# Routing of the last two batches in one pass: joint running maximum, one rescaling, one accumulated product

## The chip, the cores and the metric

The kernel runs on one core of a Trainium2 chip. The metric is the device time of one execution in microseconds. The kernel before takes 646.65 us, the median of three runs (645.55, 646.65, 647.51).

## The reference

Three layers in a row, all in float32. First a packed attention over 8 batches, 8 heads, 576 rows and head size 64: 32 packed queries attend to all rows, and then all rows attend to the 32 results. Then a soft mixture of 8 experts with 32 slots (4 per expert), and last a two-layer network with the activation h * tanh(softplus(h)). The change lies in the second layer, where the softmax of the logits runs over all 4608 rows, for each slot:

```
logits = x @ phi
d = logits - logits.max(0, keepdims=True)
d = np.exp(d)
d /= d.sum(0, keepdims=True) + 1e-09
slot_input = d.T @ x
```

After that each expert computes `relu(slot_input[e] @ w1[e]) @ w2[e]`, and the rows mix the slots by a softmax of the same logits over the 32 slots.

## The kernel before, in words

**Stages.** The kernel first does the attention batch by batch. The rows' logits of a batch (tile LT) come out of the attention weights A and a small product G of the packed values and phi, so the layer's input x is never formed. After the last batch the experts run one after the other (ex_h, ex_x, ex_o), with TensorE products of the slots against w1 and w2, then the last network over row blocks, which is the longest stage.

**Routing of a batch.** The sum over all rows is kept as a running one. For batch b the steps are: r_mx (maximum mc of LT per partition), r_mr (TensorE turns it into a row, mr), r_row (row maximum; nrep is the running negative maximum), r_d (TensorE copies it to the partitions, mp; ACT writes column b of nM), r_de (exponential dT and its sum sb), r_da (al, the factor by which older sums are rescaled), r_dt and r_dt_c (transposed dp, copied to Dt), r_u and r_u_c (product us with A, copied to up), r_sel and r_sel_c (uq, copied to U), r_si (product si with the packed values pp) and r_si_c (si_acc = al * si_acc + si). For the last batch r_last also forms the sum ss over partitions and its reciprocal rs, by which si_acc is scaled. si_acc is turned by TensorE (sit_ps) and copied to SIT, which the first expert product hp (line 986) reads.

**Order around the change.** All engines work in the order in which the kernel's code issues them (a manual schedule). The last two batches, x = 6 and y = 7, are written out as a list of calls. In it stand two kinds of filler. warm1(n) issues n products of the identity with itself, with no reader. bg(n) issues the next n steps of a fixed list: the conversion of eight w_in tiles, numbered 0 to 7, each of three steps (cv_z on ACT, line 280; cv_u on DVE, line 286; cv_m on DVE, line 289), whose results are kept in win.

**Transfers.** SP issues all weight loads in one fixed order into buffers that are used again; `done` after the last reader of a buffer lets the next load into it be written. A load waits on SP for the readers of its buffer, and the loads behind it wait with it. The buffers of w_in tiles 1 to 7 are taken, in this order, by two tiles of w1 of expert 3, four more w_in tiles and the first tile of w2 of expert 3. Behind these stand loads into the buffers of w1 of experts 0 and 1, and so on through the experts to the 16 tiles of w_out.

Of the kernel before, what the change touches and what calls it, by code (L numbers as in the profile page):

```python
# [9 lines left out]
F32 = mybir.dt.float32  # L10
F32R = mybir.dt.float32r
I32 = mybir.dt.int32
AF = mybir.ActivationFunctionType
ALU = mybir.AluOpType
# [5 lines left out]
def kernel(  # L20
# [13 lines left out]
    nc = tc.nc  # L34
    B, H, S, D = q.shape
# [269 lines left out]
    def bg(n):  # L305

        for _ in range(n):
            if bgq:
                bgq.pop(0)()
# [217 lines left out]
    def s2_mul(b, z):  # L527
        lo, hi = parts(b, z)
        A = v4(st[b]["A"][:, lo:hi])
        n = (hi - lo) * 4  # L530
        m = st[b].pop(("rs", z))
        nc.gpsimd.tensor_tensor(out=A, in0=A, in1=m[:, :, None].to_broadcast([128, n, J]), op=ALU.mult)

    def at(b, n):
        d = st[b]
        A = d["A"]
        if n == 0:
            AT = t1.tile([128, HQ, NB, 128], F32, name="AT", tag="eT", bufs=1)
            d["AT"] = AT.rearrange("p q i c -> p q (i c)")
        AT = d["AT"]  # L540
        if n < HQ:
            tp = ps_t.tile([128, 4, 128], F32, name="at", tag="t")
            for i in range(4):
                nc.tensor.transpose(tp[:, i], A[:, HQ * i + n], ident)
            nc.scalar.copy(out=AT[:, n, 0:512], in_=tp.rearrange("p i c -> p (i c)"))  # L545
            return
        rem = ps_t.tile([128, HQ, 64], F32, name="atr", tag="t")
        nc.tensor.transpose(rem.rearrange("p q c -> p (q c)"), A[:, 8], ident)
        nc.scalar.copy(out=AT[:, :, 512:576], in_=rem)
# [39 lines left out]
    def r_d(b):  # L589
        d = st[b]  # L590
        mp = ps_t.tile([128, 1], F32, name="mp", tag="t")
        nc.tensor.matmul(mp, lhsT=nrep.rearrange("p g m -> p (g m)"), rhs=ident[0:1, 0:1], start=True, stop=True)
        nc.scalar.copy(out=nM[:, b:b + 1], in_=mp)

    def r_de(b):
        d = st[b]
        dT = t1.tile([128, 192], F32, name="dT", tag="dT", bufs=1)
        sb = s_acc if b == 0 else t1.tile([128, 1], F32, name="sb", tag="sb")
        nc.scalar.activation(out=dT, in_=LT[:, b], func=AF.Exp, bias=nM[:, b:b + 1], scale=1.0, accum_out=sb)
        d["dT"] = dT  # L600
        d["sb"] = sb

    def r_da(b):
        d = st[b]
        if b:
            al = t1.tile([128, 1], F32, name="al", tag="al")
            nc.scalar.activation(out=al, in_=nM[:, b - 1:b], func=AF.Exp, bias=nM[:, b:b + 1], scale=-1.0)
            d["al"] = al

    def r_dt(b):  # L610
        d = st[b]
        dT = d.pop("dT")
        dp = ps_t.tile([128, NB, M], F32, name="dp", tag="t")
        nc.tensor.transpose(dp[:, 0:4].rearrange("p i m -> p (i m)"), dT[:, 0:128], ident)
        for hq in range(HQ):
            nc.tensor.matmul(dp[64 * hq:64 * hq + 64, 4], lhsT=dT[0:32, 128:192], rhs=ident[0:32, 0:32], start=True, stop=True)
        d["dp"] = dp

    def r_dt_c(b):
        d = st[b]  # L620
        dp = d.pop("dp")
        Dt = t1.tile([128, NB, M], F32, name="Dt", tag="Dt")
        nc.scalar.copy(out=Dt, in_=dp)
        d["Dt"] = Dt

    def r_u(b):
        d = st[b]
        A, Dt = d.pop("A"), d.pop("Dt")
        us = ps_t.tile([128, HQ * 128], F32, name="us", tag="t")
        for i in range(4):  # L630
            nc.tensor.matmul(
                us[32 * i:32 * i + 32], lhsT=Dt[:, i], rhs=A[:, HQ * i:HQ * i + HQ].rearrange("p q c -> p (q c)"),
                start=True, stop=False,
            )
        for i in range(4):
            r = slice(64 * (i // 2), 64 * (i // 2) + 64)
            nc.tensor.matmul(
                us[32 * i:32 * i + 32, 64 * i:64 * i + 64], lhsT=Dt[r, 4], rhs=A[r, 8, 64 * (i % 2):64 * (i % 2) + 64],
                start=False, stop=True,
            )  # L640
        d["us"] = us

    def r_u_c(b):
        d = st[b]
        us = d.pop("us")
        up = t1.tile([128, HQ * 128], F32, name="up", tag="up", bufs=1)
        nc.scalar.copy(out=up, in_=us)
        d["up"] = up

    def r_sel(b):  # L650
# [7 lines left out]
    def r_sel_c(b):  # L658
        d = st[b]
        uq = d.pop("uq")  # L660
        U = t1.tile([128, HQ * M], F32, name="U", tag="U")
        nc.scalar.copy(out=U, in_=uq)
        d["U"] = U

    def r_si(b):
        d = st[b]
        U, pp = d.pop("U"), d.pop("pp")
        si = ps_t.tile([128, HQ, D], F32, name="si", tag="t")
        for hq in range(HQ):
            for h4 in range(4):  # L670
                r = slice(32 * h4, 32 * h4 + 32)
                nc.tensor.matmul(si[r, hq], lhsT=U[r, hq * M:hq * M + M], rhs=pp[r, hq], start=True, stop=True)
        d["si"] = si

    def r_si_c(b):
        d = st[b]
# [11 lines left out]
    def r_last(b):  # L688

        d = st[b]  # L690
        al, sb = d.pop("al"), d.pop("sb")
        nc.vector.scalar_tensor_tensor(out=s_acc, in0=s_acc, scalar=al, in1=sb, op0=ALU.mult, op1=ALU.add)
        ss_ps = ps_t.tile([128, 1], F32, name="ss_ps", tag="t")
        nc.tensor.matmul(ss_ps, lhsT=idrep, rhs=s_acc, start=True, stop=True)
        rs = t1.tile([128, 1], F32, name="rs", tag="rs")
        nc.vector.tensor_scalar_add(out=rs, in0=ss_ps, scalar1=1e-9)
        nc.vector.reciprocal(out=rs, in_=rs)
        nc.vector.tensor_scalar(out=si_acc, in0=si_acc, scalar1=al, scalar2=rs, op0=ALU.mult, op1=ALU.mult)
        d["rs"] = rs
# [116 lines left out]
    def warm1(n):  # L816

        ps = ps_s1.tile([128, 2, 512], F32, name="s1", tag="s1")
        for _ in range(n):
            nc.tensor.matmul(ps[:, 0, 0:128], lhsT=ident, rhs=ident, start=True, stop=True)  # L820
# [67 lines left out]
    warm1(2)  # L888
    r_row(x)
    at(y, 1)  # L890
    s2_mul(y, 2)
    at(y, 2)
    r_d(x)
    bg(3)
    r_de(x)
    lt(y)
    lt_c(y)
    r_dt(x)
    warm1(4)
    r_dt_c(x)  # L900
    bg(1)
    bg(3)
    r_u(x)
    r_mx(y)
    r_mr(y)
    bg(1)
    bg(1)
    bg(1)
    warm1(4)
    warm1(1)  # L910
    r_u_c(x)
    bg(1)
    r_sel(x)
    warm1(2)
    r_sel_c(x)
    r_row(y)
    bg(1)
    bg(1)
    bg(1)
    r_d(y)  # L920
    r_da(x)
    r_si(x)
    r_de(y)
    bg(1)
    r_da(y)
    r_dt(y)
    r_dt_c(y)
    warm1(1)
    r_si_c(x)
    bg(2)  # L930
    bg(1)
    r_u(y)
    bg(1)
    r_u_c(y)
    warm1(2)
    r_last(y)
    r_sel(y)
    warm1(2)
    bg(1)
    r_sel_c(y)  # L940
    r_si(y)
    r_si_c(y)
    bg(1)


    sit_ps = ps_t.tile([128, 128], F32, name="sit_ps", tag="t")
# [592 lines left out]
```

## Time and profile before

| | before |
|---|---|
| median of three runs | 646.65 us |
| the profiled execution | 644.71 us, its span 642.9 us |
| mean granted TensorE clock in it | 0.989 of full |
| busy share of the span: PE, DVE, ACT, POOL | 95%, 78%, 53%, 9% |
| HBM read, written | 79.23 MB, 9.44 MB |

The span is cut by the profile into stages only through time: the join of the last two batches lies from about 145 to 163 us, the experts from there to about 222 us, the last network behind them. Busy shares are averages over these stages, so what an instruction costs is read in its own stretch: a timeline gives start and length of each instruction and, in brackets, how long its engine waited before it and for whom.

### The profile page before, as it was taken

Reading aid. Unit: us, or ns where it says so; the run is one execution under the profiler, and the core shown is the slowest. Engines: PE = TensorE matmul, PEld = TensorE weight load, DVE = VectorE, ACT = ScalarE, POOL = GpSimd, SP = SyncE. Lnnn points to the kernel's source line nnn. Section 1 sums busy time; section 2 is a strip of 40 time slices with the busy share of each in tenths; the row PEclk is TensorE's granted clock in tenths of the full one; section 3 lists DMA queues with packets and bytes.
Section 4 is the critical chain, followed back from the end, with each engine's and each line's share of the span. In section 5 each row is a group of like instructions: output and inputs, shape, how many; then the busy total and the mean of one; then the engine's idle time right before and its main releaser. Section 6 shows DMA issues by size and latency. Waiting matters only on the chain.

```text
span 642.9 us, 14422 instructions
## 1 busy us (share of the span) xinstructions
PE 611.3 (95%) x5874; PEld 528.6 (82%) x5874; DVE 501.1 (78%) x997; ACT 337.8 (53%) x681; POOL 55.2 (9%) x78
## 2 busy tenths in 40 slices
PE   7899999998998969999999999999999999999996
PEld 5777777776344548888899999999999999999996
DVE  5998888887564398988779987788778877887883
ACT  3345555646334367655456555555555555555551
POOL 5122222121020030010000000000000000000000
PEclk9899999998999979999999999999999999999999
DMA  8988955999999960020110110111011101110111
GB/s 283 344 292 292 343 174 199 405 413 396 360 410 412 412 223 1 1 53 14 33 34 2 34 34 2 35 34 34 2 34 34 34 2 34 34 34 2 34 34 34
DMA packets 42354, 89.61 MB, mean 139 GB/s; under 512 B 10928, under 2 KB 19248, under 8 KB 42288
## 3 DMA queue, kind: packets, MB, share of 16 engines
q1 hardware_dynamic: 41840, 88.36, 38.8%
q8 instruction: 46, 0.75, 0.5%
q10 hardware_dynamic: 192, 0.26, 0.2%
q14 instruction: 20, 0.16, 0.1%
q0 software_dynamic: 256, 0.07, 0.0%
HBM read 79.23 MB, written 9.44 MB: 138 GB/s over the span
## 4 chain that ended last, share of the span: by engine, by line
PE 65%; DVE 18%; DMA 8%; ACT 5%; issue 1%; SPq 1%; DVEq 0%; POOL 0%; ACTq 0%; POOLq 0%
PE o L1317 39%; PE so L1317 14%; DMA AW<-in_moe_w_dram 6%; PE h L1199 5%; DVE kT L335 4%; DVE A L507 1%; DMA r_wo<-in_moe_w_out_dram 1%; DVE mx L506 1%; PE s L487 1%; DVE AY L1358 1%; DVE S L1215 1%; DVE sm L522 1%; DVE nmx L383 1%; PE s L820 1%; ACT AT L545 1%
## 5 line engine op out<-in xcount | busy, mean ns | idle before, releaser
L1317 PE MATMUL o<-W,gh 128*128 128x256 f32 (+1 forms) x888 | 159.4, 306 | 0.5 <-DVE AY L1358 0.5
L1317 PEld LDWEIGHTS o<-W,gh 128*128 128x128 f32 x888 | 129.7, 190 | 10.0 <-issue 1.9
L1230 ACT CAST gh<-AY 128x512 fp32r<-128x512 f32 x116 | 53.8, 511 | 109.1 <-PE o L1317 109.1
L1204 ACT ACTIVATE AY<-h 128x512 f32<-128x512 f32 x132 | 77.1, 594 | 37.4 <-PE h L1199 36.0
L1317 PE MATMUL o<-W,gl 128*128 128x256 f32 (+1 forms) x444 | 94.3, 302 | 0.0
L1233 DVE TENSOR_TENSOR gl<-AY,gh 128x512 fp32r<-128x512 f32 x116 | 59.4, 553 | 33.0 <-ACT gh L1230 33.0
L1234 DVE TENSOR_TENSOR Sl<-S,Sh 128x1024 fp32r<-128x1024 f32 x58 | 70.9, 1223 | 10.4 <-ACT Sh L1231 9.0
L1317 PEld LDWEIGHTS o<-W,gl 128*128 128x128 f32 x444 | 70.7, 188 | 4.5
L1317 PE MATMUL o<-T,Sh 128*128 128x256 f32 x464 | 73.9, 281 | 0.4 <-DVE AY L1358 0.4
L1231 ACT CAST Sh<-S 128x1024 fp32r<-128x1024 f32 x58 | 60.8, 1049 | 5.6 <-DVE S L1215 4.3
L1317 PEld LDWEIGHTS o<-T,Sh 128*128 128x128 f32 x464 | 62.8, 189 | 0.6 <-DVE AY L1358 0.6
L1215 DVE TENSOR_TENSOR S<-AY 128x256 f32<-128x256 f32 x116 | 48.7, 420 | 9.9 <-ACT AY L1204 9.9
L1199 PE MATMUL h<-CS,W 128*128 128x256 f32 x288 | 55.7, 284 | 0.0
L1317 PE MATMUL o<-T,Sl 128*128 128x256 f32 x232 | 46.6, 282 | 0.0
L1199 PEld LDWEIGHTS h<-CS,W 128*128 128x128 f32 x288 | 43.9, 188 | 2.2 <-issue 0.7
L1358 DVE TENSOR_TENSOR AY<-AY,o 128x256 f32<-128x256 f32 x86 | 33.0, 417 | 9.4 <-PE o L1317 6.4
L1317 PE MATMUL so<-T,Sh 128*128 128x256 f32 (+1 forms) x232 | 38.7, 289 | 0.4 <-DVE AY L1358 0.4
L373 PE MATMUL s<-kT,win 128*128 128x288 f32 x128 | 34.7, 416 | 2.4 <-ACT win L385 2.3
L1317 PEld LDWEIGHTS o<-T,Sl 128*128 128x128 f32 x232 | 35.8, 190 | 0.0
L487 PE MATMUL s<-win,qT 128*128 128x128 f32 x256 | 33.7, 287 | 1.9 <-ACT win L353 1.9
L487 PEld LDWEIGHTS s<-win,qT 128*128 128x128 f32 x256 | 31.4, 200 | 2.8 <-issue 2.0
L1317 PEld LDWEIGHTS so<-T,Sh 128*128 128x128 f32 x232 | 32.5, 190 | 1.2 <-issue 0.6
(282 smaller groups left out, 1039.5 us busy)
## 6 DMA issues: line engine op xcount, KB each, us to landing
AW<-in_moe_w_dram SPq DMA_DIRECT2D x45, 512.0 KB, 10.2
r_wo<-in_moe_w_out_dram SPq DMA_DIRECT2D x16, 512.0 KB, 9.0
out_dram<-AY SPq DMA_DIRECT2D x64, 128.0 KB, 2.1
r_wi<-in_moe_w_in_dram SPq DMA_DIRECT2D x13, 512.0 KB, 8.8
AW<-in_q_dram SPq DMA_DIRECT2D x11, 576.0 KB, 5.2
AW<-in_k_dram SPq DMA_DIRECT2D x9, 576.0 KB, 7.3
AW<-in_v_dram SPq DMA_DIRECT2D x40, 128.0 KB, 5.6
AC<-in_moe_w_dram SPq DMA_DIRECT2D x10, 512.0 KB, 9.1
```

The costliest lines, as they stand in the source:

```text
L335: nc.vector.transpose(out=T[:, dh, main].rearrange("p (i r a) -> p a i r" if nm == "k" else "p (i a r) -> p a i r", i=4, a=4,), in_=x[:, 0 ...
L373: nc.tensor.matmul(ps[:, n, 0:288], lhsT=pBD[b % 2][:, hq, dh], rhs=kT[:, dh, 288 * n:288 * n + 288], start=(dh == 0), stop=(dh == 1),)
L487: nc.tensor.matmul(ps[:, k - lo], lhsT=d["qT", hq][:, dh, 64 + 128 * i:192 + 128 * i], rhs=ppBD[b % 2][:, hq, dh], start=(dh == 0), stop=( ...
L1199: nc.tensor.matmul(hp[:, 256 * f:256 * f + 256], lhsT=MS[:, 128 * ft:128 * ft + 128], rhs=CS[:, 256 * n:256 * n + 256], start=True, stop=True,
L1204: nc.scalar.activation(out=s, in_=hp.rearrange("p (f n) -> p f n", f=2), func=AF.Mish)
L1215: nc.vector.tensor_tensor(out=S[:, k], in0=x, in1=y, op=op)
L1230: nc.scalar.copy(out=gh[:, f, t], in_=s[:, f, t])
L1231: nc.scalar.copy(out=Sh, in_=S)
L1233: nc.vector.tensor_tensor(out=gl[:, f, t], in0=s[:, f, t], in1=gh[:, f, t].bitcast(F32), op=ALU.subtract)
L1234: nc.vector.tensor_tensor(out=Sl, in0=S, in1=Sh.bitcast(F32), op=ALU.subtract)
L1317: nc.tensor.matmul(o, lhsT=lhsT, rhs=rhs, start=first, stop=stop)
L1358: add = lambda o, x, y: nc.vector.tensor_tensor(out=o, in0=x, in1=y, op=ALU.add)
```

## The change

Batches 6 and 7 go through the routing together. Batch 6's exponentials use batch 7's column of nM (m in r_de), so r_mx to r_d of both come first, and r_d, r_da and r_si_c of batch 6 alone are dropped. The one factor al that is left rescales from batch 5's maximum to batch 7's. r_si takes both batches and adds their products in PSUM. r_last adds both sums. Three copies of batch 6 (Dt, up, U) move from ACT to DVE, and its dT and up lie in the tile e1. The fillers stand at other places.

```
--- before.py
+++ after.py
@@ -594,9 +594,14 @@
 
     def r_de(b):
         d = st[b]
-        dT = t1.tile([128, 192], F32, name="dT", tag="dT", bufs=1)
+        if b == B - 2:
+            d["x"] = t1.tile([128, S], F32, name="e1", tag="e1", bufs=1)
+            dT = d["x"][:, 0:192]
+        else:
+            dT = t1.tile([128, 192], F32, name="dT", tag="dT", bufs=1)
         sb = s_acc if b == 0 else t1.tile([128, 1], F32, name="sb", tag="sb")
-        nc.scalar.activation(out=dT, in_=LT[:, b], func=AF.Exp, bias=nM[:, b:b + 1], scale=1.0, accum_out=sb)
+        m = max(b, B - 1 if b == B - 2 else 0)
+        nc.scalar.activation(out=dT, in_=LT[:, b], func=AF.Exp, bias=nM[:, m:m + 1], scale=1.0, accum_out=sb)
         d["dT"] = dT
         d["sb"] = sb
 
@@ -604,7 +609,8 @@
         d = st[b]
         if b:
             al = t1.tile([128, 1], F32, name="al", tag="al")
-            nc.scalar.activation(out=al, in_=nM[:, b - 1:b], func=AF.Exp, bias=nM[:, b:b + 1], scale=-1.0)
+            a = b - 2 if b == B - 1 else b - 1
+            nc.scalar.activation(out=al, in_=nM[:, a:a + 1], func=AF.Exp, bias=nM[:, b:b + 1], scale=-1.0)
             d["al"] = al
 
     def r_dt(b):
@@ -620,7 +626,7 @@
         d = st[b]
         dp = d.pop("dp")
         Dt = t1.tile([128, NB, M], F32, name="Dt", tag="Dt")
-        nc.scalar.copy(out=Dt, in_=dp)
+        (nc.vector.tensor_copy if b == B - 2 else nc.scalar.copy)(out=Dt, in_=dp)
         d["Dt"] = Dt
 
     def r_u(b):
@@ -643,8 +649,12 @@
     def r_u_c(b):
         d = st[b]
         us = d.pop("us")
-        up = t1.tile([128, HQ * 128], F32, name="up", tag="up", bufs=1)
-        nc.scalar.copy(out=up, in_=us)
+        if b == B - 2:
+            up = d["x"][:, 192:192 + HQ * 128]
+            nc.vector.tensor_copy(out=up, in_=us)
+        else:
+            up = t1.tile([128, HQ * 128], F32, name="up", tag="up", bufs=1)
+            nc.scalar.copy(out=up, in_=us)
         d["up"] = up
 
     def r_sel(b):
@@ -659,18 +669,20 @@
         d = st[b]
         uq = d.pop("uq")
         U = t1.tile([128, HQ * M], F32, name="U", tag="U")
-        nc.scalar.copy(out=U, in_=uq)
+        (nc.vector.tensor_copy if b == B - 2 else nc.scalar.copy)(out=U, in_=uq)
         d["U"] = U
 
-    def r_si(b):
-        d = st[b]
-        U, pp = d.pop("U"), d.pop("pp")
+    def r_si(*bs):
         si = ps_t.tile([128, HQ, D], F32, name="si", tag="t")
         for hq in range(HQ):
             for h4 in range(4):
                 r = slice(32 * h4, 32 * h4 + 32)
-                nc.tensor.matmul(si[r, hq], lhsT=U[r, hq * M:hq * M + M], rhs=pp[r, hq], start=True, stop=True)
-        d["si"] = si
+                for b in bs:
+                    nc.tensor.matmul(
+                        si[r, hq], lhsT=st[b]["U"][r, hq * M:hq * M + M], rhs=st[b]["pp"][r, hq],
+                        start=(b == bs[0]), stop=(b == bs[-1]),
+                    )
+        st[bs[-1]]["si"] = si
 
     def r_si_c(b):
         d = st[b]
@@ -688,8 +700,11 @@
     def r_last(b):
 
         d = st[b]
-        al, sb = d.pop("al"), d.pop("sb")
-        nc.vector.scalar_tensor_tensor(out=s_acc, in0=s_acc, scalar=al, in1=sb, op0=ALU.mult, op1=ALU.add)
+        al = d.pop("al")
+        nc.vector.scalar_tensor_tensor(
+            out=s_acc, in0=s_acc, scalar=al, in1=st[b - 1].pop("sb"), op0=ALU.mult, op1=ALU.add,
+        )
+        nc.vector.tensor_add(out=s_acc, in0=s_acc, in1=d.pop("sb"))
         ss_ps = ps_t.tile([128, 1], F32, name="ss_ps", tag="t")
         nc.tensor.matmul(ss_ps, lhsT=idrep, rhs=s_acc, start=True, stop=True)
         rs = t1.tile([128, 1], F32, name="rs", tag="rs")
@@ -888,59 +903,50 @@
     warm1(2)
     r_row(x)
     at(y, 1)
+    warm1(2)
     s2_mul(y, 2)
     at(y, 2)
-    r_d(x)
     bg(3)
-    r_de(x)
+    bg(2)
     lt(y)
     lt_c(y)
-    r_dt(x)
-    warm1(4)
-    r_dt_c(x)
+    r_mx(y)
     bg(1)
-    bg(3)
-    r_u(x)
-    r_mx(y)
+    bg(1)
+    warm1(3)
     r_mr(y)
     bg(1)
     bg(1)
-    bg(1)
-    warm1(4)
-    warm1(1)
-    r_u_c(x)
-    bg(1)
-    r_sel(x)
-    warm1(2)
-    r_sel_c(x)
+    warm1(3)
     r_row(y)
     bg(1)
     bg(1)
-    bg(1)
     r_d(y)
-    r_da(x)
-    r_si(x)
+    warm1(4)
+    r_de(x)
     r_de(y)
-    bg(1)
     r_da(y)
+    r_dt(x)
+    r_dt_c(x)
+    warm1(1)
     r_dt(y)
     r_dt_c(y)
     warm1(1)
-    r_si_c(x)
+    r_u(x)
+    r_u_c(x)
+    r_last(y)
+    r_u(y)
+    r_u_c(y)
+    r_sel(x)
+    r_sel_c(x)
+    warm1(1)
+    r_sel(y)
+    r_sel_c(y)
+    bg(1)
+    warm1(1)
+    r_si(x, y)
+    r_si_c(y)
     bg(2)
-    bg(1)
-    r_u(y)
-    bg(1)
-    r_u_c(y)
-    warm1(2)
-    r_last(y)
-    r_sel(y)
-    warm1(2)
-    bg(1)
-    r_sel_c(y)
-    r_si(y)
-    r_si_c(y)
-    bg(1)
 
 
     sit_ps = ps_t.tile([128, 128], F32, name="sit_ps", tag="t")
```

On DVE, at the end of the join: r_wi_1 to r_wi_3 are the w_in tiles 5 to 7 here, win_92 and win_93 the results of tiles 4 to 7. Before:

```order
L286 TENSOR_SCALAR r_wi_1_1059<-r_wi_1_1059 128x512
L289 SCALAR_TENSOR_TENSOR win_92<-win_92,r_wi_1_1059 128x512
L685 SCALAR_TENSOR_TENSOR si_acc<-si_acc,al,si 128x128
L686 SCALAR_TENSOR_TENSOR s_acc<-s_acc,al,sb 128x1
L286 TENSOR_SCALAR r_wi_2_1089<-r_wi_2_1089 128x512
L289 SCALAR_TENSOR_TENSOR win_93<-win_93,r_wi_2_1089 128x512
L286 TENSOR_SCALAR r_wi_3_1144<-r_wi_3_1144 128x512
L692 SCALAR_TENSOR_TENSOR s_acc<-s_acc,al,sb 128x1
L696 TENSOR_SCALAR rs<-ss_ps 128x1
L697 RECIPROCAL rs<-rs 128x1
L698 TENSOR_SCALAR si_acc<-si_acc,al,rs 128x128
L289 SCALAR_TENSOR_TENSOR win_93<-win_93,r_wi_3_1144 128x512
```

Now:

```order
L712 RECIPROCAL rs<-rs 128x1
L713 TENSOR_SCALAR si_acc<-si_acc,al,rs 128x128
L672 COPY U<-uq 128x64
L289 SCALAR_TENSOR_TENSOR win_92<-win_92,r_wi_0_983 128x512
L694 SCALAR_TENSOR_TENSOR si_acc<-si,rs,si_acc 128x128
L286 TENSOR_SCALAR r_wi_1_1059<-r_wi_1_1059 128x512
L961 COPY SIT<-sit_ps 128x128
L289 SCALAR_TENSOR_TENSOR win_92<-win_92,r_wi_1_1059 128x512
L286 TENSOR_SCALAR r_wi_2_1089<-r_wi_2_1089 128x512
L289 SCALAR_TENSOR_TENSOR win_93<-win_93,r_wi_2_1089 128x512
L286 TENSOR_SCALAR r_wi_3_1144<-r_wi_3_1144 128x512
L289 SCALAR_TENSOR_TENSOR win_93<-win_93,r_wi_3_1144 128x512
```

The last steps of tiles 4 to 7 (L289 on win_92 and win_93) stood between the steps of the routing; now that of tile 4 stands behind the copy U, and those of tiles 5 to 7 behind the copy SIT.

On TensorE, from the fillers in the middle of the join to the us product of batch 7 before, and to ss now (s is the tile of the fillers, x4 their number; e_2235 is dT of batch 6). Before:

```order
L820 MATMUL s_2238<-ident 128x128 x4
L820 MATMUL s_2243<-ident 128x128
L655 MATMUL uq<-ids,up 128x32 x2
L820 MATMUL s_2251<-ident 128x128 x2
L592 MATMUL mp<-ident,nrep 128x1
L672 MATMUL si<-pp,U 32x64 x8
L614 MATMUL dp<-ident,dT 128x128
L616 MATMUL dp<-ident,dT 64x32 x2
L820 MATMUL s_2292<-ident 128x128
L631 MATMUL us<-A,Dt 32x256 x4
L637 MATMUL us<-A,Dt 32x64 x4
L820 MATMUL s_2313<-ident 128x128 x2
```

Now:

```order
L835 MATMUL s_2218<-ident 128x128 x3
L592 MATMUL mp<-ident,nrep 128x1
L835 MATMUL s_2230<-ident 128x128 x4
L620 MATMUL dp<-ident,e_2235 128x128
L622 MATMUL dp<-ident,e_2235 64x32 x2
L835 MATMUL s_2249<-ident 128x128
L620 MATMUL dp<-ident,dT 128x128
L622 MATMUL dp<-ident,dT 64x32 x2
L835 MATMUL s_2257<-ident 128x128
L637 MATMUL us<-A,Dt 32x256 x4
L643 MATMUL us<-A,Dt 32x64 x4
L709 MATMUL ss_ps<-s_acc,idrep 128x1
```

The row mp of batch 7 stood behind batch 6's us, mr and uq and eleven fillers; now it stands behind mr and three fillers, and both batches' dp and us follow it, with ss of r_last between the two us.

## Rows read from the trace of the kernel before

**Rows 1.** Stretches of 5 us; last columns granted TensorE clock, DMA share, GB/s.

```profile
130.00:135.00 5.00, 5.00 (x48) 4.45 (x46) 4.24 (x11) 1.84 (x8) 0.00 (x0) 1.00 1.03 416
...
150.00:155.00 5.00, 4.57 (x36) 3.20 (x37) 2.71 (x8) 3.00 (x9) 0.00 (x0) 0.66 1.02 408
...
165.00:170.00 5.00, 5.00 (x56) 1.88 (x48) 1.07 (x3) 2.73 (x3) 0.00 (x0) 1.00 0.90 297
...
170.00:175.00 5.00, 5.00 (x54) 1.79 (x56) 4.25 (x13) 1.58 (x4) 0.20 (x1) 1.00 1.01 374
```

**Rows 2.** Chain of waits from 90 to 260 us: start, length, what.

```profile
163.38 3.64 PE hp L986 x32
...
174.00 10.20 DMA AW<-in_moe_w_dram
...
214.05 8.36 DMA r_wo<-in_moe_w_out_dram
```

**Rows 3.** Timeline of SP, 152 to 167 us: seven transfers, start and length of issue.

```profile
152.66 0.33 SPq L167 DMA_DIRECT2D r_wi<-in_moe_w_in_dram  x1
...
155.82 0.33 SPq L167 DMA_DIRECT2D r_wi<-in_moe_w_in_dram  x1
...
156.96 0.33 SPq L167 DMA_DIRECT2D r_wi<-in_moe_w_in_dram  x1
...
159.35 0.33 SPq L167 DMA_DIRECT2D r_wi<-in_moe_w_in_dram  x1
...
162.12 0.38 SPq L156 DMA_DIRECT2D r_w<-in_moe_w_dram  x1
...
165.37 0.38 SPq L156 DMA_DIRECT2D AC<-in_moe_w_dram  x1
...
167.03 0.37 SPq L156 DMA_DIRECT2D AW<-in_moe_w_dram  x1
```

**Rows 4.** Landing times: those issued at 152.66, 165.37, 167.03; all of w_out.

```profile
r_wi<-in_moe_w_in_dram SPq DMA_DIRECT2D x1, 512.0 KB, 10.6
...
AC<-in_moe_w_dram SPq DMA_DIRECT2D x1, 512.0 KB, 4.2
...
AW<-in_moe_w_dram SPq DMA_DIRECT2D x1, 512.0 KB, 5.0
...
DMA to landing us min/median/max: 3.4/9.0/10.4
```

**Rows 5.** Timeline of DVE, 150 to 155 us, and its conversions (min/median/max ns).

```profile
150.73 0.35 DVE L572 TENSOR_REDUCE mc<-AY 128x1 f32<-128x192 f32 x1
...
154.91 0.28 DVE L585 SCALAR_TENSOR_TENSOR nrep<-row,nrep 1x128 f32<-1x128 f32 x1
...
L286 DVE TENSOR_SCALAR r_wi<-r_wi x13: 409/422/433, 148.5 to 205.3; 128x512 int32<-128x512 int32 x13
...
L289 DVE SCALAR_TENSOR_TENSOR win<-win,r_wi x7: 674/692/694, 149.0 to 161.4; 128x512 int32<-128x512 int32 x7
```

**Rows 6.** Timeline of PE (TensorE), 150 to 162 us: start, length, instruction.

```profile
150.93 1.95 PE L820 MATMUL s<-ident 128*128 128x128 f32 x8
...
152.81 1.08 PE L631 MATMUL us<-A,Dt 128*32 128x256 f32 x8
...
156.86 0.38 PE L592 MATMUL mp<-ident,nrep 1*128 1x1 f32 x2
...
158.11 0.33 PE L614 MATMUL dp<-ident,dT 128*128 128x128 f32 x1 [0.52 <-ACT dT L599]
...
159.07 0.64 PE L631 MATMUL us<-A,Dt 128*32 128x256 f32 x8
...
161.64 0.43 PE L672 MATMUL si<-pp,U 32*32 32x64 f32 x16
```

**Rows 7.** Timeline of ACT, 157 us.

```profile
157.27 0.16 ACT L593 COPY nM<-mp 128x1 f32<-128x1 f32 x1
...
157.53 0.44 ACT L599 ACTIVATE dT<-AY,nM 128x192 f32<-128x192 f32 x1
```

## The prediction

> **What bounds the kernel now.** I read the stretches first, then the chain of waits, then the queue of transfers on SP, and last the engines between 150 and 164 us. In the stretches the reader is to see the DMA column: before the join 416 GB/s move at a share of 1.03, and the only hole in the loading of weights is 297 GB/s from 165 to 170 us and 374 from 170 to 175 [rows 1]. The chain agrees: from 174.00 to 222.41 us it runs through DMA landings almost without a break, and the TensorE work of the join ends in front of that, where the first expert product (hp) starts at 163.38 [rows 2]. So **the stream of weights sets the end of this stage**. Engine time saved in the join counts only as far as they let bytes flow sooner, and that can happen only where the stream starves now.
>
> Why it starves is in SP's queue [rows 3]. A transfer there waits until the buffer that it overwrites has been read, and all later ones wait behind it. I number them: t9 (issued 152.66), t10 (155.82), t11 (156.96), t12 (159.35) and t13 (162.12) each wait for the last DVE step of one early w_in conversion (indices 3 to 7); t14 (165.37) waits for expert 0's first product to be done with w1, and t15 (167.03) for expert 1's. One transfer is 512 KB, at 416 GB/s 1.26 us. t9 lands at 152.66 + 10.6 = 163.26 [rows 3, 4]; at full pace t14 is due five steps later, at 169.56, and does land at 165.37 + 4.2 = 169.57. t15 would be due at 170.83 but lands at 167.03 + 5.0 = 172.03: **1.2 us late**. That is the hole, and it is most of what this change can win.
>
> **The change, the engines.** Before, batch 6 went through the whole routing alone and batch 7 behind it; now both go through it together, with batch 7's running maximum.
>
> *Up to nM.* The 128x1 maximum mc started at 150.73 [rows 5] and starts about then still: two weight conversions are now ahead of LT's copy on ACT, but mc stood behind conversions on DVE before. Two more fillers stand ahead of atr, in a wait of TensorE that was there anyway. mc (0.35) and mr end at about 151.4. DVE then has 0.69 + 0.42 + 0.69 of conversions ahead of row and nrep (0.28 each) [rows 5], so nrep ends at about 153.2, where it started at 154.91. mp then goes at about 153.25; before, it stood on TensorE behind eleven fillers, us, uq and mr, the first part at half clock, until 156.86 [rows 6]. **Gain so far: 3.6 us.**
>
> *From nM on.* Before, mp to nM took 0.41 us, and dT to dp 0.58 [rows 6, 7]. One exponential (al) between nM and dT is gone, so dT(6) starts at about 153.85 and dp(6) at 154.45, with the four fillers ahead of it in that wait. Now two of each stand in line: dp, filler, dp, filler (dp to us took 0.96 with a wait for the copy of Dt inside [rows 6]; I take 0.5 for a dp and 0.25 for a filler), us(6) at about 155.95. The us product takes 0.64 plus its remainder, 0.9 in all. Then ss waits for DVE: the 128x256 copy of us, which now stands ahead of the sums, at 0.4 (between mc's 0.35 for 192 columns and a conversion's 0.42 for 512 [rows 5]), two one-column sums, and the hand-offs: ss at about 157.65, and us(7) queued behind it until 157.8. us(7) 0.9, uq 0.4, filler, uq 0.4, filler: si at about 160.0. From si to hp it was 163.38 - 161.64 = 1.74 us [rows 2, 6]; si now has 32 instructions for 16, another 0.43. **hp at about 162.15, a gain of 1.25 us.** The tail gives back 2.35 of the 3.6, since both batches now pass it in one line. The rescaling of batch 6 alone that is dropped (one si_acc and one s_acc update on DVE, one al on ACT, one filler group) is counted in the new line of work; nothing else waited for it.
>
> **The change, the transfers.** This is where the sum is made. Conversions 4 to 7 have left the middle of the join. The last step of 4 now stands behind U's copy on DVE, at about 159.3 to 160.0; that of 5 behind the copy SIT that releases hp, at 162.15 to 162.8; 6 and 7 follow at 0.42 + 0.69 - their overlap, about 1.05 us each. So t10 goes at 160.1 (due 164.5), t11 at about 162.85 (due 165.8), t12 at 163.9, t13 at 164.95; t14 and t15 come 1.25 us sooner than before and directly behind. The shortage thus moves from t15 to t11, which is issued 2.95 us before it is due, where t15 had 3.8. SP has no other work behind these waits, but the rest of expert 3 and every later expert stand there.
>
> How late t11 is depends on how fast a 512 KB transfer lands in a thin queue, which the trace bounds [rows 4]: 3.4 us is the shortest of any such load (w_out), 4.2 is t14's, 5.0 is t15's. t11 then lands at 166.25, 167.05 or 167.85, late by 0.45, 1.25 or 2.05; t12 and t13 follow at pace. Against the 1.2 us lost now, that is -0.75, +0.05 or +0.85. I take 4.6, halfway between the two that went through the same thin queue, and get **+0.45 us**. Behind 222 us nothing is touched.
>
> The Trainium skill, "DMA: Bandwidth & Descriptors", section "Anatomy of one DMA — SWDGE (gpsimd) path", fits a transfer of that path as about 2.0 us fixed plus its bytes at 436 GB/s; taken over to SP's queue, as an estimate, that makes 3.2 us for these: by that t11 would be late by 0.25 and the sum -0.95. The trace does not agree for this stretch: t14 took 4.2 and t15 5.0, with two or three others unfinished.
>
> Summed against the profiled execution: 644.71 + 0.45 = 645.2. That one lies 1.94 us under the median of the three runs, 646.65; against the median the forecast is 646.65 + 0.45 = **647.1 us, no change that can be measured** (0.3%, 1.9 us, is about what a measurement of this kernel can tell).
>
> **The rivals.**
>
> *1. Slower: TensorE's clock falls in the new line of dp and us.* From 150 to 155 us the granted clock averaged 0.66, so it was at the lower of its levels (1.2 instead of 2.4 GHz) for 0.34 x 5 / 0.5 = 3.4 us, after waits of TensorE for dT and for atr; four fillers then took 1.95 and us 1.08 where it took 0.64 later [rows 1, 6]. The new order has a wait of over 1 us between its fillers and mp, with nothing to fill it. If such a stretch begins by the time dp(6) starts, two fillers cost about 0.5 more, us 0.6 and two dp 0.3: hp at 163.55, t11 issued at 164.25, landing (4.2 to 5.0 later) 2.65 to 3.45 late, so +1.45 to +2.25 us: **648.5**. For it: the fall before, and that t11 hangs on the end of the join. Against it: more fillers stand before mr than did. It decides from the clock being down at dp.
>
> *2. A little faster: a thin queue lands as fast as the shortest load.* With 3.4 us t11 is late by 0.45 and the kernel gains 0.75: **645.9**. For it: the 3.4 is measured; t11 has only two transfers before it. Against it: t14 and t15. The rule of the Trainium skill named above is this case with 3.2 us.
>
> *3. Clearly faster: the hole closes altogether.* If the stream has enough in flight with the earlier t14 to t18, all that 165 to 175 us now lack comes back: (416 - 297) x 5 + (416 - 374) x 5 = 805 KB, 1.9 us at 416 GB/s [rows 1]: **644.7**. Against it: t10 to t13 all go 2.8 to 5.9 us later than they did.
>
> **How the numbers follow.** Forecast (landing in 4.2 to 5.0 us, +0.05 to +0.85): 0.50. Rival 1: 0.22. Rival 2: 0.16. Rival 3: 0.12. All of the forecast and of rival 2 is within 0.3%; of rival 1 somewhat under half lies beyond +1.9, and a clock lowered for longer adds some: slower 0.15. Rival 3 is just at the bound; with the scatter of three runs I give faster 0.13, and no change 0.72. The range runs from 645.0, between rivals 3 and 2, to 648.7, within the upper half of rival 1; what is left out is about half of rival 3 and a third of rival 1, under 0.2.
>
> **What would show it.** Right: mp of batch 7 near 153.3, hp near 162.1, and yet landings from 174 us on at about the old times; on SP a gap from about 153 to 160, t11 behind the SIT copy, and GB/s falling between 160 and 167 us instead of 165 to 170. Wrong: no DMA hole at all and the w_out landings over 1 us sooner (rival 3); a clock of 0.5 between 154 and 158 and hp not sooner (rival 1). The forecast is also wrong if hp is sooner and the end of the stage follows it by the same 1.25 us, for then TensorE and not the stream was the bound.

## The result, and the profile after

The change takes 650.48 us, the median of 11 runs (648.66 to 653.12); the kernel before, run beside it, 645.55 (11 runs, 644.10 to 647.51). The ratio is 1.008, interval 1.006 to 1.0099: **slower by about 4.9 us**, where 647.1, that is +0.45 over the 646.65 known then, was forecast.

| | before | after |
|---|---|---|
| the profiled execution, its span | 644.71, 642.9 us | 649.5, 647.7 us |
| mean granted TensorE clock in it | 0.989 | 0.989 |
| busy PE, DVE | 95%, 78% | 95%, 77% |
| start of batch 7's mp, counted from batch 6's mc | 11.44 us | 7.77 us |
| start of hp, from the same mc | 17.96 us | 17.16 us |
| copy SOT of the experts' result, from the same mc | 74.79 us | 77.34 us |

The last three rows are counted from the start of mc of batch 6 (145.42 us before, 146.01 after), because the stages ahead of it, which the change leaves as they were, end at 145.4 to 148.0 us in the profiles of this study (145.6 to 147.1 for the change alone). All marks below are counted so.

The engines first. Timeline of PE, the change, 150 to 164 us (start, length, instruction, in brackets the wait before it):

```profile
151.61 0.27 PE L577 MATMUL mr<-ident,mc 128*1 128x128 f32 x1 [0.52 <-DVE mc L572]
...
153.78 0.38 PE L592 MATMUL mp<-ident,nrep 1*128 1x1 f32 x2 [1.23 <-DVE nrep L585]
...
156.69 0.64 PE L637 MATMUL us<-A,Dt 128*32 128x256 f32 x8
...
158.45 0.38 PE L709 MATMUL ss_ps<-s_acc,idrep 128*128 128x1 f32 x2 [0.87 <-DVE s_acc L707]
...
161.11 0.75 PE L681 MATMUL si<-pp,U 32*32 32x64 f32 x32
...
163.17 0.63 PE L992 MATMUL hp<-AY,SIT 128*32 128x512 f32 x3 [0.40 <-DVE SIT L961]
```

mp goes 3.7 us sooner after mc than in [rows 6], and hp only 0.8. So in this pair of profiles the engines did nearly what was forecast. Now the bytes, in stretches of 5 us (last columns granted clock, DMA share, GB/s), the change:

```profile
155.00:160.00 5.00, 4.13 (x55) 2.51 (x53) 1.70 (x7) 1.14 (x5) 0.00 (x0) 1.00 1.04 417
160.00:165.00 5.00, 4.14 (x70) 2.52 (x73) 3.58 (x9) 1.41 (x4) 0.00 (x0) 1.00 0.78 261
165.00:170.00 5.00, 5.00 (x59) 1.88 (x51) 2.16 (x6) 2.95 (x3) 0.00 (x0) 1.00 0.72 233
170.00:175.00 5.00, 5.00 (x56) 1.79 (x60) 4.23 (x13) 1.58 (x4) 0.39 (x1) 1.00 1.05 396
```

The hole of [rows 1] has moved forward and become deeper: 261 and 233 GB/s where 391 and 297 flowed. The row of the kernel before, which [rows 1] leaves out:

```profile
160.00:165.00 5.00, 4.13 (x54) 2.64 (x58) 1.91 (x6) 0.58 (x2) 0.00 (x0) 1.00 1.02 391
```

What opens the hole is on DVE, the last steps of conversions 4 to 7 in the change (timeline, start and length):

```profile
160.39 0.68 DVE L289 SCALAR_TENSOR_TENSOR win<-win,r_wi 128x512 int32<-128x512 int32 x1
...
162.82 0.29 DVE L961 COPY SIT<-sit_ps 128x128 f32<-128x128 f32 x1 [0.22 <-PE sit_ps L955]
163.03 0.68 DVE L289 SCALAR_TENSOR_TENSOR win<-win,r_wi 128x512 int32<-128x512 int32 x1
...
164.16 0.69 DVE L289 SCALAR_TENSOR_TENSOR win<-win,r_wi 128x512 int32<-128x512 int32 x1
...
165.30 0.71 DVE L289 SCALAR_TENSOR_TENSOR win<-win,r_wi 128x512 int32<-128x512 int32 x1
```

On SP the transfers t10 to t13 follow each of these at once (timeline, start and length of issue; behind it the time to landing of the same four, from the DMA view of one issue each):

```profile
161.13 0.33 SPq L167 DMA_DIRECT2D r_wi<-in_moe_w_in_dram  x1
163.78 0.33 SPq L167 DMA_DIRECT2D r_wi<-in_moe_w_in_dram  x1
164.89 0.33 SPq L167 DMA_DIRECT2D r_wi<-in_moe_w_in_dram  x1
166.04 0.38 SPq L156 DMA_DIRECT2D r_w<-in_moe_w_dram  x1
```

```profile
r_wi<-in_moe_w_in_dram SPq DMA_DIRECT2D x1, 512.0 KB, 4.1
r_wi<-in_moe_w_in_dram SPq DMA_DIRECT2D x1, 512.0 KB, 4.6
r_wi<-in_moe_w_in_dram SPq DMA_DIRECT2D x1, 512.0 KB, 5.3
r_w<-in_moe_w_dram SPq DMA_DIRECT2D x1, 512.0 KB, 6.2
```

Landings, issue plus latency: t9 163.71, t10 165.23, t11 168.38, t12 170.19, t13 172.24, t14 174.21, t15 175.42. From t9 to t15 that is 11.71 us, where it was 172.03 - 163.26 = 8.77 before [rows 3, 4]: **2.94 us lost in the stream**. The chain of the change runs through it: behind hp it goes from one landing to the next.

```profile
163.17 3.64 PE hp L992 x32
...
167.53 9.19 DMA AW<-in_moe_w_dram
176.74 10.78 DMA AW<-in_moe_w_dram
```

At SOT 77.34 - 74.79 = 2.55 of the 2.94 are left. The two spans differ by 4.8 us: 0.59 lie ahead of mc, in stages that the change leaves as they were, 2.55 between mc and SOT, and 1.66 behind SOT. Of the 4.9 us between the medians some 2 are then still without a cause.

### The profile page after: what moved, and what is told of

Read it like the earlier page. It is cut to its first block, busy times and chain, and to the rows that moved or that the text cites. A ratio compares the mean times of both kernels' runs of the same rounds, so it can differ in the third digit from the quotient of the medians.

```text
span 647.7 us, 14412 instructions
## 1 busy us (share of the span) xinstructions
PE 613.5 (95%) x5872; PEld 527.9 (82%) x5872; DVE 501.1 (77%) x999; ACT 336.4 (52%) x676; POOL 56.4 (9%) x78
## 4 chain that ended last, share of the span: by engine, by line
PE 67%; DVE 18%; DMA 8%; ACT 4%; issue 1%; SPq 0%; DVEq 0%; POOL 0%; ACTq 0%; POOLq 0%
PE o L1323 39%; PE so L1323 13%; DMA AW<-in_moe_w_dram 6%; PE h L1205 5%; DVE kT L335 4%; DVE A L507 1%; DVE mx L506 1%; PE s L487 1%; DVE AY L1364 1%; DVE S L1221 1%; DVE nmx L383 1%; DMA AC<-in_k_dram 1%; ACT AT L545 1%; PE hp L992 1%; DVE sm L522 1%
## 5 line engine op out<-in xcount | busy, mean ns | idle before, releaser
L1323 PE MATMUL so<-W,Sh 128*128 128x256 f32 x208 | 33.0, 281 | 0.0
```

The source lines that it names most:

```text
L1323: nc.tensor.matmul(o, lhsT=lhsT, rhs=rhs, start=first, stop=stop)
```

## The experiments

**Conversions against routing.** Theory S: the conversions that have gone late starve the stream. Theory J: the joint routing itself costs the time. Three kernels take them apart, and share the kernel before (645.98 us, 29 runs, 643.44 to 652.07).

*e1*: the change, with conversions 4 to 7 put back into waits of DVE and ACT in the joint routing.

```
     bg(1)
+    bg(1)
     r_d(y)
...
     r_da(y)
+    bg(2)
     r_dt(x)
...
     r_dt_c(y)
+    bg(4)
     warm1(1)
...
     r_last(y)
+    bg(1)
...
     r_si_c(y)
-    bg(2)
```

> The change with one part undone: the last steps of the w_in conversions 4 to 7 go back into the waits of DVE and ACT inside the join (4 and 5 before Dt, 5 to 7 behind Dt and behind rs), the joint routing stays. Theory S (the stream of weights starves because the buffers of tiles 4 to 7 come free late): t10 to t13 are issued near 155, 157, 158 and 161 us instead of 161.1, 163.8, 164.9 and 166.0, the hole of 160 to 170 us goes, and the kernel takes 645 us, between 1 us under and 0.5 over the kernel before. Theory J (the joint routing itself or its fillers cost the time, through TensorE's clock or the longer line from nM to SIT): the time stays near 650.

*e2*: the kernel before, with the steps of conversions 4 to 7 taken out of the middle of the join and put behind r_sel_c(y) (on DVE that is behind rs) and behind SIT; the routing is the old one.

```
     r_row(y)
-    bg(1)
-    bg(1)
-    bg(1)
     r_d(y)
...
     r_de(y)
-    bg(1)
     r_da(y)
...
     r_si_c(x)
-    bg(2)
-    bg(1)
     r_u(y)
-    bg(1)
...
-    bg(1)
     r_sel_c(y)
+    bg(1)
     r_si(y)
     r_si_c(y)
-    bg(1)
+    bg(2)
```

> The kernel before with only that part done: its two routings stay apart, but the last steps of the conversions 4 to 7 stand where the change has them, behind rs and behind the copy SIT. Theory S: t10 is issued near 162 and t11 to t13 near 164 to 166, the stream has the same hole or a somewhat larger one (hp is 0.8 us later than in the change), and the kernel is slower than before by 3 to 5 us, 649 to 651. Theory J: no more than 1 us slower than before.

*e3*: the change, with 4 and 5 early and 6 and 7 late: the first two additions of e1, a bg(1) in place of its bg(4), and the later steps all behind SIT.

> The change with conversions 4 and 5 back inside the join and 6 and 7 left behind the copy SIT, so t10 and t11 go early (155 and 157) and t12 and t13 near 164 and 165. Theory S with a thin queue: t12 is due near 167.5 and lands 4.6 us after its issue, 1 to 1.5 late, so the loss lies between that of the first kernel and that of the change: 646 to 648. If t10 and t11 alone were the cause, 645; if the hole had another cause, 650.

| | median us (runs) | ratio to before, interval | SOT from mc |
|---|---|---|---|
| e1 | 648.59 (12) | 1.0027, 0.9998 to 1.0055 | 74.37 us |
| e2 | 648.05 (12) | 1.0011, 0.9983 to 1.0039 | 77.73 us |
| e3 | 651.61 (12) | 1.0062, 1.0028 to 1.0096 | 77.17 us |

The ratio, with its 95% interval, is not the quotient of the two medians. Stretches of e1, then of e2:

```profile
160.00:165.00 5.00, 4.14 (x74) 2.93 (x78) 2.47 (x8) 0.58 (x2) 0.00 (x0) 1.00 1.02 407
165.00:170.00 5.00, 5.00 (x56) 1.72 (x52) 0.74 (x2) 2.02 (x2) 0.00 (x0) 1.00 1.02 388
```

```profile
160.00:165.00 5.00, 4.14 (x68) 2.87 (x57) 2.24 (x9) 2.69 (x10) 0.00 (x0) 1.00 0.81 325
165.00:170.00 5.00, 4.47 (x52) 1.80 (x56) 3.40 (x8) 1.35 (x3) 0.00 (x0) 1.00 0.66 200
```

By the marks S holds: the joint routing with early conversions keeps 407 and 388 GB/s and reaches SOT at 74.37, level with the kernel before; the old routing with late ones has the change's hole and reaches it 2.9 later. Two late conversions (e3) cost 2.4, nearly as much as four. But the times don't follow the marks, and all three expected times were missed: e1 should have been level with before and its median lies 2.6 above; e2 should have been 3 to 5 us slower and is not shown to be slower (its interval holds 1); e3 should have come at 646 to 648 and is the slowest of the three. Something else differs between executions.

*e4*: e1, with the line from dp to si shortened (four single fillers out, of which the cut shows one; r_last behind the second us). With it the kernel before again twice, and the change again, each for one more execution with a profile (theory C: behind SOT the difference is only where a fall of the clock happens to lie; "the first product of the last network" in these texts is the first product o of its second layer, line 1317 before).

```
     bg(4)
-    warm1(1)
     r_u(x)
     r_u_c(x)
-    r_last(y)
-    bg(1)
     r_u(y)
     r_u_c(y)
+    r_last(y)
+    bg(1)
```

> The first experiment (joint routing, conversions early) with a shorter line from nM to SIT: the four single fillers between the two dp, us, uq and si are dropped, and ss of both batches goes behind the second us instead of between the two, so that the second us runs while DVE copies the first. Theory S: the buffers of tiles 4 to 7 still come free early, and hp comes 1.5 to 2 us sooner than in the first experiment, so t14 and t15 are no longer late; counted from the maximum of batch 6, SOT comes at 73 to 73.8 us where the kernel before has 74.8 and the first experiment 74.4, and the kernel gains 1 to 1.8 us, 644 to 645. If TensorE's clock falls for want of the fillers, hp comes no sooner than in the first experiment and nothing is gained. If the loading of weights were not what binds, SOT would follow hp by the full 2.5 us against the kernel before.

> The kernel before once more, for a second profile of its own. Theory C (the 1.5 us that all four other profiles lose between the copy SOT and the first product of the last network is the phase of the clock's fall, no part of the change): in some looks at the kernel before the granted clock also falls within about 1.2 us of SOT, and SOT to the first product then takes 16.3 to 16.5 us instead of 15.0. If it belongs to the change, the kernel before always shows 15.0.

> The same as the look before it, again: 15.0 us from SOT to the first product where the clock stays up behind SOT, 16.3 to 16.5 where it falls there. From the maximum of batch 6 to SOT 74.5 to 75.1 us in either case, if the stream of weights sets that stretch.

> The change once more. From the maximum of batch 6 to SOT 77.0 to 77.7 us (theory S: the stream's hole is the same in every execution); behind SOT 15.0 or 16.5 us by theory C, depending on where the clock falls, and always 16.5 if that part belongs to the change.

e4 took 649.19 us (9 runs, 645.77 to 651.86), ratio 1.0052 (1.0031 to 1.0073), though its profiled execution has a span of 644.0. That execution misses its marks too: hp came at 16.12, 1.0 us sooner than in e1 where 1.5 to 2 was expected, and SOT at 75.98 instead of 73 to 73.8. Its clock was at the lower level from 161.64 to 165.06 us, in which hp itself runs (1.07 us where the change has 0.63), and t15 was issued only 21.3 us after mc (19.9 in e5 below, which has the same line):

```profile
161.98 1.07 PE L991 MATMUL hp<-AY,SIT 128*32 128x512 f32 x3 [0.39 <-DVE SIT L960]
```

The three single executions took 648.97 and 646.17 (before) and 649.46 (the change). What parts the two of the kernel before is the granted clock in the join. PE of the second of them, which has no fall there (timeline, 148 to 163 us):

```profile
151.05 1.16 PE L820 MATMUL s<-ident 128*128 128x128 f32 x8
...
155.48 0.38 PE L592 MATMUL mp<-ident,nrep 1*128 1x1 f32 x2
...
162.01 0.63 PE L986 MATMUL hp<-AY,SIT 128*32 128x512 f32 x3 [0.39 <-DVE SIT L955]
```

Here the fillers take 1.16 us, not 1.95 [rows 6], and hp comes 16.47 us after mc, not 17.96. The execution that the prediction was read from thus held a fall that cost its join 1.5 us, and the stream hid it: SOT is at 74.64 and 74.79. In the first of the two the clock was at the lower level from 157.25 to 167.5 (an expectation below calls it the second); hp came at 19.30 and SOT at 77.60, so the 74.5 to 75.1 expected for SOT in either case holds only without such a stretch.

**Where the clock falls.** Over all executions of this study (222, each with its mean granted clock) a straight line with one slope and an offset for each kernel gives 4.1 us for each 0.01 of the mean clock, with 1.05 us of scatter left. So e4 and the change were each run twice more with a profile. Theory C2: the medians come from executions with long low stretches in the join.

> The joint routing with early conversions and a shorter line, unchanged, one more execution with a profile. Over all runs so far the time follows the granted clock: 4.1 us for each 0.01 of the mean clock, and at equal clock this kernel lies with the one before; its median was higher since 6 of its 9 runs had a mean clock of 0.976 to 0.981. Theory C2 (low clock in more places): if this run's mean clock is 0.981 or lower, the time is 648.5 to 652 and a stretch of about 10 us at the lower level shows in or behind the join (145 to 170 us), as in the second look at the kernel before (157.25 to 167.5); if it is 0.989, the time is 645.5 to 647.5 and no such stretch is there. Theory J (the joint routing costs time by itself): 649 or more at 0.989 too.

> As e4_again_1, another execution. Theory C2: 645.5 to 647.5 at a mean clock of 0.989, 648.5 to 652 at 0.981 or lower, the low stretch between 145 and 170 us. Theory J: 649 or more at any clock.

> The change, unchanged, one more execution with a profile. Theory S (stream): the copy SOT comes 76.9 to 77.7 us after the start of batch 6's mc, as in the two executions seen, against 74.6 to 74.8 in the kernel before without a fall of the clock in its join. Theory C2: 649 to 650 us at a mean clock of 0.989, 651.5 to 653 at 0.979 to 0.982, and then a longer low stretch in the join than in the first two.

> As a_again_2, another execution: SOT 76.9 to 77.7 us after mc by theory S; 649 to 650 us at 0.989, 651.5 to 653 at 0.979 to 0.982 by theory C2.

e4 took 648.79 and 648.47 us, both at a clock of 0.981, with the lower level from 158.29 to 168.53 and from 158.25 to 168.50. With the first (161.64 to 165.06) and one beside e5 (157.09 to 167.33) all four profiles of e4 hold a fall in the join. The change took 652.02 (0.981, low from 158.49 to 168.73) and 649.26 (0.988, no fall in the join). With the later runs beside e7 (below) five executions of the change have a profile:

| execution of the change | clock low in the join | hp from mc | SOT from mc | time |
|---|---|---|---|---|
| first profile | never | 17.16 | 77.34 | 649.50 |
| a_again_1 | 162.78 to 166.19 | 17.13 | 77.64 | 649.46 |
| a_again_2 | 158.49 to 168.73 | 19.71 | 79.99 | 652.02 |
| a_again_3 | never | 17.13 | 77.59 | 649.26 |
| a_on_same_chip | 154.25 to 171.31 | 22.13 | 82.52 | 654.60 |

The table bears C2 out: the two long stretches go with the two longest times. Theory S's 76.9 to 77.7 for SOT holds only in the three others; behind a long stretch SOT came at 79.99 and 82.52. The last one in stretches:

```profile
155.00:160.00 5.00, 4.71 (x34) 2.64 (x33) 0.55 (x2) 0.69 (x4) 0.00 (x0) 0.50 1.02 410
160.00:165.00 5.00, 4.43 (x30) 3.43 (x30) 1.98 (x8) 0.53 (x3) 0.00 (x0) 0.50 0.35 138
165.00:170.00 5.00, 4.10 (x54) 2.06 (x57) 2.91 (x7) 1.17 (x3) 0.00 (x0) 0.50 0.38 115
```

The clock is at the lower of its levels all through, and the hole falls to 115 GB/s, since conversions 5 to 7 stand behind a SIT that comes 5 us later (t11 was issued at 168.62).

**Waits or chance.** Theory W: the clock falls because TensorE stands idle in the new waits. Theory P: the falls come whatever stands there.

*e5*: e4 with 15 more fillers in the waits.

```
     gmat_c(y)
-    warm1(1)
+    warm1(4)
...
-    warm1(3)
+    warm1(5)
     r_mr(y)
     bg(1)
     bg(1)
-    warm1(3)
+    warm1(8)
     r_row(y)
...
+    warm1(3)
     r_last(y)
...
     r_si(x, y)
+    warm1(2)
     r_si_c(y)
```

> The joint routing with early conversions and the shorter line (e4), with 15 more fillers in the waits of TensorE in the join: 3 ahead of mr of batch 6, 2 ahead of mr of batch 7, 5 ahead of mp, 3 ahead of ss, 2 ahead of the turn of si_acc; mp, us and hp start as before. Theory W (the clock falls in the join since TensorE stands idle in the new waits; the falls make the median): the mean clock of its executions is 0.986 to 0.990, not 0.976 to 0.981 as in most of e4, and the median is 645.5 to 647, level with the kernel before. Theory P (the falls in the join come whatever stands there, by chance): the clocks and the median stay as in e4, 648 to 650. In both SOT comes 74.4 to 76 us after mc where the clock does not fall in the join.

*e6*: e4 without warm1(3) ahead of r_mr(y), warm1(3) ahead of r_row(y) and warm1(4) behind r_d(y). *e4 once more* beside them, and the kernel before (646.04 us, 29 runs).

> e4 without the three groups of fillers between the maximum of batch 7 and dp (3, 3 and 4): the opposite step to e5. Theory W: more and longer falls, mean clock mostly 0.976 to 0.981 or lower, median 649 to 651. Theory P: as e4, 648 to 650, with a share of executions at 0.989.

> e4 again beside e5 and e6, for the share of its executions with a fall in the join: by its first 9 and the 2 looks, 8 of 11 at a clock of 0.981 or lower; median 648 to 650 by either theory, and 645.5 to 647.5 in the executions at 0.989.

| | median us (12 runs each) | ratio to before, interval | mean clock of the executions |
|---|---|---|---|
| e6, fewest fillers | 649.52 | 1.0048, 1.0017 to 1.0078 | 0.973 to 0.984 |
| e4 | 648.28 | 1.003, 1.0003 to 1.0058 | 0.978 to 0.986 |
| e5, most fillers | 645.49 | 0.9988, 0.9964 to 1.0013 | 0.988 to 0.994 |

PE of e6 (timeline; the waits ahead of mr, mp and dp), then of e5, where mr and mp wait for nothing:

```profile
151.41 0.27 PE L577 MATMUL mr<-ident,mc 128*1 128x128 f32 x1 [1.44 <-DVE mc L572]
153.57 0.55 PE L592 MATMUL mp<-ident,nrep 1*128 1x1 f32 x2 [1.90 <-DVE nrep L585]
154.95 0.48 PE L620 MATMUL dp<-ident,e 128*128 128x128 f32 x1 [0.83 <-ACT e L604]
...
156.48 1.08 PE L637 MATMUL us<-A,Dt 128*32 128x256 f32 x8
```

```profile
151.51 0.27 PE L577 MATMUL mr<-ident,mc 128*1 128x128 f32 x1
151.62 1.95 PE L835 MATMUL s<-ident 128*128 128x128 f32 x16
153.67 0.38 PE L592 MATMUL mp<-ident,nrep 1*128 1x1 f32 x2
...
155.91 0.64 PE L637 MATMUL us<-A,Dt 128*32 128x256 f32 x8
```

In e6 us takes 1.08 us and hp comes at 18.92; in e5 it takes 0.64 and hp comes at 16.21, with the same routing. W holds, and by the medians too: products that nobody reads are worth 2.8 us here (648.28 against 645.49). SOT came at 75.32 in this execution of e5 and at 73.56 in another (below), neither with a fall in the join, so the mark itself varies by 1.8 us between executions of one kernel. The two groups stay apart all the same: over the profiles without a fall of 10 us or more in the join, SOT lies at 77.17 to 77.73 with late conversions (six) and at 73.56 to 75.98 with early ones (six, the kernel before among them).

**Both causes weighed in the change.** *e7*: the change with the 15 fillers in the same five places, conversions late. Beside it the change and e5 (before: 645.00 us, 24 runs).

> The change as it is (conversions 4 to 7 late) with the 15 fillers of e5 in the same waits of TensorE. Theories S and W together: its executions have a mean clock of 0.986 to 0.99, so the part that the clock costs goes and the part that the stream costs stays: median 648 to 649.5, 2 to 3.5 over the kernel before, SOT 76.9 to 77.7 us after mc. If the clock were all: 645.5 to 646.5, as e5. If the stream were all: as the change on the same chip.

> The change beside e7: median 649.5 to 651, clocks 0.979 to 0.989.

> e5 beside e7, which differs in the place of conversions 4 to 7 and in the shorter line: median 645 to 646.5, clocks 0.988 to 0.994; e7 less e5 is what the late buffers cost, 2 to 3.5 us by theory S.

| | fillers in the waits | conversions | median us (runs) | ratio to before, interval | SOT from mc |
|---|---|---|---|---|---|
| the change | few | late | 651.56 (9) | 1.0087, 1.0056 to 1.0117 | 82.52 us |
| e7 | more | late | 649.14 (10) | 1.0063, 1.0039 to 1.0086 | 77.43 us |
| e5 | more | early | 644.06 (12) | 0.9984, 0.9960 to 1.0009 | 73.56 us |

The 82.52 is from the execution with the 17 us stretch. Stretches of e7, then of e5 beside it:

```profile
160.00:165.00 5.00, 4.61 (x80) 3.28 (x76) 3.15 (x9) 1.71 (x4) 0.00 (x0) 1.00 0.89 338
165.00:170.00 5.00, 5.00 (x60) 1.72 (x52) 2.52 (x6) 2.03 (x2) 0.00 (x0) 1.00 0.71 195
```

```profile
160.00:165.00 5.00, 4.61 (x73) 2.03 (x62) 0.98 (x3) 1.01 (x1) 0.00 (x0) 1.00 1.01 389
165.00:170.00 5.00, 5.00 (x60) 2.10 (x56) 2.55 (x6) 2.02 (x2) 0.00 (x0) 1.00 1.03 386
```

Filling the waits gives the change 2.4 us and leaves it 4.1 slower than the kernel before (2 to 3.5 was expected). Beside it the change came out 0.6 us slower and e5 0.9 us faster than their expectations. The step from e7 to e5 is 5.1, more than the 2 to 3.5 expected: e5's executions lie mostly at 0.994 and e7's at 0.989 (0.005, by the slope 2.1 us), and e5 has the shorter line too, so some 3 us are left for the buffers and the line together. By the straight line at equal clock, less the kernel before, with two standard errors: the change +2.8 ± 0.5, e7 +3.8 ± 0.7, e2 +2.6 ± 0.7, e3 +2.8 ± 0.7 (late conversions); e1 +0.8 ± 0.7, e4 -0.6 ± 0.6, e5 0.0 ± 0.5, e6 -1.1 ± 0.8 (early). The two pairs that differ in nothing but the conversions give 2.0 ± 0.8 (the change less e1) and 2.6 ± 0.7 (e2 less the kernel before): that is what the late buffers cost. e5 is the best version; that it beats the kernel before isn't shown, since both of its intervals hold 1.

## Why the prediction was wrong

**Right.** That the weight stream sets the end of the stage and that engine time alone gains nothing; the marks bear it out: in two profiles of the kernel before hp lies 1.5 us apart and SOT 0.15. That the shortage moves forward from t15 to t11 (it then lasted to 170 us and not to 167). That t11 stands behind SIT. It landed 4.6 us after its issue, the value taken, but that was luck: in three other executions of the change it took 3.3, 3.6 and 3.6. mp: 3.67 us sooner after mc, where 3.6 was said; the terms as written (conversions, row and nrep behind the end of mr at 151.4) add to 153.8 and not to 153.2, but on DVE the conversions ran beside mr.

**The step that failed: "t12 and t13 follow at pace".** Pace was 1.26 us. t12, t13 and t14 landed 1.81, 2.05 and 1.97 us behind one another, 2.05 us more than pace in all, though issued 0.47 to 1.15 us apart. t10 and t11 gave 2.15 together (t10 0.26, t11 1.89) where 1.65 was taken and 2.05 was the far end. The sum is then 2.15 + 2.05 - 0.05 (t15) = 4.15 us behind pace, less the 1.21 lost before, +2.94 where +0.45 stood. The price was put on one transfer, and all three behind it paid too. The prediction gives no reason for the term. In the trace that it was read from, the hole was one late transfer, and the three behind it, issued 0.5 us apart, did come at pace (1.37, 1.21 and 1.21 us); in the change conversions feed the queue, one load each 1.1 us. Measured from t10 to t14 the late kernels need 8.98 us (the change; 8.02 in a_again_1), 9.48 (e7) and 8.77 (e2), the kernel before 5.15.

Which load pays differs between executions. Issue and time to landing of t11 and t12 in a_again_1:

```profile
163.33 0.33 SPq L167 DMA_DIRECT2D r_wi<-in_moe_w_in_dram  x1
164.43 0.33 SPq L167 DMA_DIRECT2D r_wi<-in_moe_w_in_dram  x1
```

```profile
r_wi<-in_moe_w_in_dram SPq DMA_DIRECT2D x1, 512.0 KB, 3.3
r_wi<-in_moe_w_in_dram SPq DMA_DIRECT2D x1, 512.0 KB, 6.1
```

Here t11 was only 0.3 us late, and t12 landed 3.9 us behind it. From t9 to t15 this execution took 10.63 us and a_again_3 11.98, 1.9 and 3.2 more than the kernel before, and SOT came at 77.64 and 77.59, as in the first profile. So no price for t11 alone could have given the sum.

**The second cause** was rival 1, put at 0.22 and at 1.45 to 2.25 us. It was priced as one stretch of 3.4 us at the lower level, as in [rows 1]. The change's own profile shows no fall in the join, and yet the mechanism is real: others of its executions have one of 10 us (hp +2.6, SOT +2.5 us against the other three) or 17 us (+5.0 and +5.0). A mean clock of 0.984 or less is found in 12 of 23 executions of the change, 14 of 94 of the kernel before, and none of the 34 of e5 and e7. The mean clock does not say where a fall lies; that only the profiles do. The median clocks of the change and of the kernel before, 0.984 and 0.989, make 0.005, by the slope 2.1 us: with the 2.8 at equal clock the 4.9 that were measured. The rival was right to name the wait of over 1 us ahead of mp, which is 1.23, and wrong in treating the fall as a thing that a single profile decides; it is a share of the executions.

The Trainium skill, "TensorE: Matmul & The Clock Gate", section "Part 1: The HAM clock gate (the "warmup" mystery)", states that the window over which activity is watched runs freely, so that the same kernel has a different number of slow products at its start from run to run. That executions of one kernel differ, the five of the change bear out, though in the middle of the kernel (low for 0 to 17 us in the join, 649.26 to 654.60 us); whether a free-running window is the reason, no run here shows.

**The gain at hp** was 0.8 us for 1.25, and even that is owed to the fall in the profile of before. Against its execution without one (hp at 16.47) the change's 17.13 to 17.16 is 0.7 *later*: the one line, as built, was longer than the two routings behind one another. e4 and e5, without its four single fillers and with ss behind the second us, reach hp at 16.12 and 16.21. mp's gain shrinks likewise, from 3.67 to 9.94 - 7.77 = 2.2. Row 1's clock of 0.66 was read, and used for rival 1 alone; it should also have been taken out of the base.

**Rivals 2 and 3** needed the stream to be as good as before or better. Rival 2's condition, a landing of t11 in 3.4 us, was met in a_again_1 (3.3), and SOT was as late as ever, since the price lay in the transfers behind. The 3.2 us that the prediction estimated from the section "Anatomy of one DMA — SWDGE (gpsimd) path" of the Trainium skill's "DMA: Bandwidth & Descriptors" was reached by no load from t10 to t15 of the late kernels; that 3.3 is the shortest.

## What to carry to other kernels

When the last reader of a load's buffer moves, write down the new issue time of every load behind it, and price the whole run of thin-queue landings, not the first alone. In a chain with waits, read the clock of several executions before calling any stretch of the base normal, and price a fall as a chance times a length. When an edit takes work out of TensorE's waits, try fillers there: from e4 to e5 they were worth 2.8 us.

## What the runs showed of the hardware that was not expected

Loads of 512 KB that entered a nearly dry queue 0.5 to 1.15 us apart landed 1.8 to 2.05 us apart (t12 to t14 of the change), at 233 GB/s and a DMA share of 0.72, where a full queue lands one each 1.26 at 416 [rows 1]. With the old routing (e2) it is much the same, 200 GB/s from 165 to 170 us at a share of 0.66. Why the share stays below 1 although four loads were unfinished at 166.6 us and six at 168 (by issue and landing) was not settled.

The clock went to its lower level in the join after waits of TensorE of 0.5 to 1.23 us with products between them, in some executions and not in others of one kernel; e6, with waits of 1.44 and 1.90, had a mean clock of 0.984 or less in all of its 12. A second place is just at or behind SOT: from SOT to the first product o of the last network's second layer 14.99 us passed in the profile of before, without a fall there, 17.34 and 16.43 in its two other executions and 16.52 in the first profile of the change, with one. Theory C holds by this, though the 17.34 lies beyond the 16.3 to 16.5 expected: most of the 1.66 us that the first pair of profiles differs by behind SOT is where the clock fell. What decides the place in a single execution stays open.
